# Transposes ahead of two weight chunks in the load queue of a fused LayerNorm + MLP kernel

## Chip, cores, metric

One core of a Trainium2 chip. The metric is the device time of one execution in microseconds (us), median over the runs. The verdicts use runs of the fast state alone. The profile's span is the time from the first to the last instruction; the device time is 1.7 to 2.1 us longer.

## The reference

```python
B, S, D, F = 1, 2048, 1024, 3584          # bf16
def reference(x, w1, b1, w2, b2):
    y = _layernorm(x, axis=-1)
    h = _gelu(jnp.einsum("bsd,df->bsf", y, w1) + b1)
    return jnp.einsum("bsf,fd->bsd", h, w2) + b2
```

## The kernel before

Both matrix products are done as 2x2 block products with seven products instead of eight (Winograd's form), so PE (TensorE) saves an eighth of the work, and DVE (VectorE) pays with sums of blocks of y, w1 and w2. The kernel writes down tasks with dependencies and a due time. A small planner inside it simulates the engines, and so fixes the order of each engine and of the load queue; a packer with a random seed places the buffers.

At the start, y comes into being: 16 tiles of x (128 tokens each) are normalised and transposed. Tiles 0 to 3 are transposed on PE, tiles 4 to 7 by DMA. Until the sums T of y exist, PE can only make products q1 and q2 (which use plain blocks), so it makes them for the first RH = 11 rows of w1, ahead of all else:

```python
RH = 11                    # rows that run ahead of the sums
WAVE_ROWS = 7              # rows in the first wave, token tile by token tile
...
for ch in range((RH + 1) // 2):          # upper half of w1, two rows a chunk, two loads each
    w1_load(0, ch, "A1", (None, W_DUE[ch]) if ch < len(W_DUE) else None)
for i in range(4):
    pr.due = (None, HEAD_LN[i]); norm(i)
... # dummy products keep PE busy
for t in range(4):                       # the first wave: 128-column products
    wave(t, range(0, 3)); ...
    if t < 3: to_yT_pe(0, t + 1, ((7, 0, 8, "ACT", 2),))
    wave(t, range(3, WAVE_ROWS) if t else range(3, 6))
for i in range(4, 8): norm(i)
...
for i in range(4, 8):                    # DMA transposes and the sums T of y
    due(lambda: (to_yT_dma(0, i), tsum(0, i - 4)), HEAD_DUE[0] + HEAD_DUE[1] * (i - 4))()
for r in range(RH):                      # 15 full products: q1 of rows 7-10, q2 of rows 0-10
    if r + 1 >= WAVE_ROWS and r + 1 < RH: p1(r + 1)
    p2(r)
    ...
warm(1, bank=7, full=True)
for ch in range(2):
    if ch == 0: w1_load(0, 0, "A2")      # lower half of w1, first chunk
    w1_sums(0, ch)
# then q6 of row 0, the first product that needs a T and a sum of w1
```

Each `w1_load` is two DMAs of 256 KB. The last product before the sums is q2 of row 10; its weights are the second load of the last upper chunk.

## Time and profile before

| | before |
|---|---|
| device time | 333.53 us median of 3 (333.23 to 334.26) |
| profiled run | 334.5 us, span 332.8 us |
| PE busy | 326.4 us (98%) |
| longest PE wait after the head | 1.42 us, for the sums of y |

The prediction below shows the page's engine row, the chain and PE's timeline. The list of who waited for whom, for PE alone (engine and line, what it waited for: us in total, times, longest), adds that nothing else holds PE after the head:

```profile
PE ps L929 <- DVE mem L758: 1.4, 1, 1.4
PE ps L1301 <- PEq L1596: 0.8, 1, 0.8
PE ps L1346 <- DVE mem L724: 0.5, 1, 0.5
PE ps L1301 <- DVE st_sb L683: 0.4, 1, 0.4
```

L758 is the sums of y, L724 an eviction of tile 0's transpose, L1301 the dummy products.

### The profile page before, as it was taken

How to read it: one execution, taken by the hardware profiler on the slowest of the kernel's cores; microseconds unless marked ns; L12 is line 12 of the kernel's file. 1: busy time of each engine (PE TensorE's matmuls, PEld its weight loads, DVE VectorE, ACT ScalarE, POOL GpSimd, SP SyncE). 2: the span in 40 equal slices, each digit the busy share in tenths (PEclk: the TensorE clock that was granted, in tenths of full speed). 3: DMA queues.
4: the chain of work that ended last, by engine and by line, in shares of the span. 5: the costliest groups of instructions: out<-in, count | busy, mean ns of one | idle time of the engine just before them, and what ended most of it. 6: DMA issues, size and time to landing. Idle time of an engine off the chain costs nothing.

```text
span 332.8 us, 4669 instructions
## 1 busy us (share of the span) xinstructions
PE 326.4 (98%) x1672; PEld 153.9 (46%) x1673; DVE 299.9 (90%) x479; ACT 179.7 (54%) x307; POOL 15.2 (5%) x31
## 2 busy tenths in 40 slices
PE   7998999999999999999999999999999999999996
PEld 4843444444444444444444444444444444444445
DVE  5969999999999986996999997989999999899984
ACT  4795999997577676677675553561211214211411
POOL 2310122111000000000000000000000000000000
PEclk9999999999999999999999999999999999999999
DMA  8998897999998989999967564555689867999768
GB/s 232 323 191 230 246 291 181 301 240 276 306 316 304 318 262 347 315 350 368 320 200 226 152 180 118 161 166 167 175 223 256 228 201 197 279 279 274 186 125 195
DMA packets 121184, 80.73 MB, mean 243 GB/s; under 512 B 35146, under 2 KB 112586, under 8 KB 121162
## 3 DMA queue, kind: packets, MB, share of 16 engines
q1 hardware_dynamic: 118106, 79.32, 84.9%
q10 hardware_dynamic: 3056, 1.11, 1.3%
q8 instruction: 13, 0.21, 0.3%
q14 instruction: 9, 0.07, 0.1%
HBM read 48.70 MB, written 24.38 MB: 220 GB/s over the span
## 4 chain that ended last, share of the span: by engine, by line
PE 90%; SPq 4%; DMA 3%; DVE 1%; issue 0%
PE ps L929 45%; PE ps L1271 44%; SPq L782 3%; DMA mem<-mem 2%; DMA mem<-in_w_dram 1%; DVE mem L758 1%; SPq L653 1%; PE ps L1278 1%; SPq L1319 0%; PE ps L1151 0%; DVE mem L1240 0%; SPq L650 0%; SPq L1320 0%
## 5 line engine op out<-in xcount | busy, mean ns | idle before, releaser
L929 PE MATMUL ps<-mem 128*128 128x512 f16 x756 | 164.1, 379 | 1.4 <-DVE mem L758 1.4
L1271 PE MATMUL ps<-mem 128*128 128x512 f16 x672 | 145.7, 379 | 0.0
L929 PEld LDWEIGHTS ps<-mem 128*128 128x128 f16 (+1 forms) x756 | 73.5, 98 | 91.0 <-DVE mem L758 1.7
L854 ACT COPY mem<-ps 128x512 f32<-128x512 f32 x111 | 64.5, 588 | 75.5 <-PE ps L1271 61.3
L1271 PEld LDWEIGHTS ps<-mem 128*128 128x128 f16 (+1 forms) x672 | 65.7, 98 | 79.3
L838 ACT ACTIVATE mem<-ps,b_sb 128x512 f16<-128x512 f32 x112 | 73.1, 692 | 24.4 <-DVE ps L862 13.8
L862 DVE TENSOR_TENSOR ps<-ps,mem 128x512 f32<-128x512 f32 x84 | 58.0, 693 | 7.4 <-ACT mem L854 4.7
L1086 DVE TENSOR_TENSOR mem<-mem 128x2048 f16<-128x2048 f16 (+1 forms) x56 | 59.3, 1083 | 3.2 <-PE ps L1271 2.4
L794 DVE TENSOR_TENSOR mem<-mem 128x1024 f16<-128x1024 bf16 (+1 forms) x56 | 38.0, 684 | 5.0 <-DMA mem<-in_w_dram 3.6
L995 DVE TENSOR_TENSOR mem<-mem 128x512 f16<-128x512 f16 (+5 forms) x84 | 37.0, 460 | 1.5 <-DMA mem<-in_w_dram 1.1
L1098 DVE TENSOR_TENSOR mem<-mem 128x2048 f16<-128x2048 f16 (+1 forms) x32 | 33.5, 1082 | 1.2 <-PE ps L1271 1.2
L845 ACT COPY ps<-ps 128x512 f32<-128x512 f32 x31 | 17.7, 570 | 24.2 <-DVE mem L1170 15.0
L683 DVE BATCH_NORM_STATS2 st_sb<-mem 128x6 f32<-128x512 bf16 x24 | 15.3, 673 | 3.6 <-DMA mem<-in_x_dram 3.5
L1170 DVE TENSOR_TENSOR mem<-ps,mem 128x512 f32<-128x512 f32 x24 | 16.4, 682 | 1.3 <-PE ps L1271 1.1
L979 DVE TENSOR_TENSOR mem<-mem 128x2048 f16<-128x2048 bf16 (+1 forms) x16 | 17.2, 1077 | 0.1
L1123 DVE TENSOR_TENSOR mem<-ps,mem 128x512 bf16<-128x512 f32 x22 | 14.8, 682 | 0.9 <-PE ps L1271 0.8
L758 DVE TENSOR_TENSOR mem<-mem 128x512 f16<-128x512 f16 x32 | 11.9, 417 | 1.7 <-DMA mem<-mem 1.6
L687 POOL TENSOR_TENSOR rstd_sb<-mv_sb,nhalf 128x1 f32<-128x1 f32 x12 | 8.5, 711 | 45.7 <-DVE mv_sb L685 45.6
L1346 PE MATMUL ps<-mem 128*128 128x128 f16 x112 | 7.3, 219 | 0.6 <-DVE mem L724 0.5
L690 DVE TENSOR_SCALAR mem<-mem,mv_sb,rstd_sb 128x1024 f16<-128x1024 bf16 (+1 forms) x13 | 6.6, 515 | 1.3 <-POOL rstd_sb L687 1.2
L1257 ACT COPY ps<-b_sb 128x512 f32<-128x512 f32 x6 | 3.5, 588 | 7.6 <-DVE mem L1170 7.5
L1346 PEld LDWEIGHTS ps<-mem 128*128 128x128 bf16 x112 | 6.4, 98 | 1.0 <-DVE mem L724 0.7
(45 smaller groups left out, 73.0 us busy)
## 6 DMA issues: line engine op xcount, KB each, us to landing
mem<-in_w_dram SPq DMA_DIRECT2D x80, 256.0 KB, 4.8
mem<-w_scr SPq DMA_DIRECT2D x28, 448.0 KB, 3.8
w_scr<-mem SPq DMA_DIRECT2D x21, 512.0 KB, 5.2
w_raw<-mem SPq DMA_DIRECT2D x12, 512.0 KB, 4.9
mem<-w_raw SPq DMA_DIRECT2D x12, 448.0 KB, 4.4
mem<-in_w_dram SPq DMA_DIRECT2D x9, 448.0 KB, 4.0
mem<-in_x_dram SPq DMA_DIRECT2D x15, 256.0 KB, 4.5
out_dram<-mem SPq DMA_DIRECT2D x12, 256.0 KB, 4.0
```

What stands on the lines that cost most here:

```text
L794: op("DVE", d_tt(n), lambda e: e.tensor_tensor(out=o[0], in0=a[0], in1=bb[0], op=f), r=[a[1], bb[1]], w=[o[1]], name=f"w1S{k}_{ch}")
L838: op("ACT", A_GELU, lambda e: e.activation(out=dst, in_=banks[bank][:, :], func=ACT.Gelu_apprx_tanh, bias=b1_sb[:, f:f + 1], scale=1.0), r ...
L845: op("ACT", A_CP, lambda e: e.copy(out=banks[dst][:, :], in_=banks[src][:, :]), r=[bank_c[src]], w=[bank_c[dst]], name=name, lat=A_LAT)
L854: op("ACT", A_CP, lambda e: e.copy(out=v16(a, 0, 2048, F32), in_=banks[src][:, :]), r=[bank_c[src]], w=[a.c()], name=name, lat=A_LAT)
L862: op("DVE", D_PS, lambda e: e.tensor_tensor(out=banks[dst][:, :], in0=banks[src][:, :], in1=v16(a, 0, 2048, F32), op=ALU.add), r=[bank_c[s ...
L929: i = e.matmul(banks[bank][:, :], lhsT=lv[:, k, :], rhs=rv[:, k, :], start=(fresh and k == 0), stop=(k == KH - 1), skip_group_check=True)
L979: op("DVE", d_tt(2 * self.n), lambda e: e.tensor_tensor(out=vd, in0=va, in1=vb, op=ALU.subtract), r=self.cells(a) + self.cells(bb), w=self ...
L995: tt = lambda o, a, c: (lambda e: e.tensor_tensor(out=o, in0=a, in1=c, op=ALU.subtract))
L1086: op("DVE", d_tt((k1 - k0) * 512), lambda e, a=a, bb=bb, o=o: e.tensor_tensor(out=o, in0=a[0], in1=bb[0], op=f), r=a[1] + bb[1], w=[t.c(z) ...
L1098: op("DVE", d_tt((k1 - k0) * 512), lambda e, va=va, vb=vb, vd=vd: e.tensor_tensor(out=vd, in0=va, in1=vb, op=f), r=h_cells(b, a, s, k0, k1 ...
L1170: op("DVE", D_PS, lambda e: e.tensor_tensor(out=av(dst), in0=banks[bank][:, :], in1=av(src), op=ALU.add), r=[bank_c[bank], src.c()], w=[ds ...
L1271: i = e.matmul(banks[bank][:, :], lhsT=bv[:, k, :], rhs=av3[:, k, :], start=(fresh and k == 0), stop=(k == KQ - 1), skip_group_check=True)
```

## The change

The intent: the transposes of tiles 4 to 7 stood in the queue behind the upper chunks of w1 and the first lower chunk. The last upper chunk and the first lower one now depend on the end of the first wave, so the transposes go first. The head's due times, the planner's price of a transpose, a limit on the planner's queue and the packing seed are tuned with it. The core of the diff (three changes of the same cost factor, to 1.9, are cut to one):

```diff
+BACKLOG = 4.5
...
+                        if e == "SP" and dma_free - now > BACKLOG + 1e-6:
+                            heapq.heappush(events, dma_free - BACKLOG)
+                            break
...
-SEED = 22
+SEED = 18
-HEAD_DUE = (2.0, 1.2)
-HEAD_LN = (4.4, 7.6, 11.1, 12.2)
-TE_DUE = 7.4
-T0_PARTS = ((7, 0, 2, "DVE", 1), (5, 2, 4, "DVE", 1), (6, 4, 8, "ACT", 1))
-W_DUE = (5.5, 9.0)
+HEAD_DUE = (4.0, 2.0)
+HEAD_LN = (3.4, 5.8, 10.2, 14.0)
+TE_DUE = 5.6
+T0_PARTS = ((7, 0, 2, "ACT", 1), (5, 2, 4, "DVE", 1), (6, 4, 8, "ACT", 1))
+W_DUE = (6.2, 7.0)
+W_GATE = (3, 3)
...
-                    ..., P * D * 2 * 1.3, None, f"Td{i}")     # the planner's price of a transpose
+                    ..., P * D * 2 * 1.9, None, f"Td{i}")
...
-            for ch in range((RH + 1) // 2):
+            for ch in range((RH + 1) // 2 - 1):
                 w1_load(0, ch, "A1", ...)
...
                 wave(t, range(3, WAVE_ROWS) if t else range(3, 6))
+                if t == W_GATE[0]:
+                    gate[0] = pr.last_pe
+                    w1_load(0, (RH + 1) // 2 - 1, "A1")
+                    gate[0] = None
+                if t == W_GATE[1]:
+                    gate[0] = pr.last_pe
+                    w1_load(0, 0, "A2")
+                    gate[0] = None
...
-                if ch == 0:
-                    w1_load(0, 0, "A2")
```

More of the change, by code (lines that the diff above doesn't have):

```diff
@@ L740, in to_yT_dma @@
                 dma("SP", lambda e: e.dma_start_transpose(dst, v16(xbuf)),
-                    [xbuf.c(0), xbuf.c(1)], [y[b, c].c((0, t)), y[b, c].c((1, t))], P * D * 2 * 1.3, None, f"Td{i}")
+                    [xbuf.c(0), xbuf.c(1)], [y[b, c].c((0, t)), y[b, c].c((1, t))], P * D * 2 * 1.9, None, f"Td{i}")
                 M.free(xbuf)
@@ L1135, in finish @@
                     dma("SP", lambda e: e.dma_start_transpose(v3(t, 0, t.n, n, BF16), v16(o, 0, o.n, BF16)),
-                        [o.c(0), o.c(1)] if how == "both" else [o.c(dt)], [t.c()], P * o.n * 2.2, None, f"To{i}{k}{u}{v}")
+                        [o.c(0), o.c(1)] if how == "both" else [o.c(dt)], [t.c()], P * o.n * 1.9, None, f"To{i}{k}{u}{v}")
                     M.free(o)
@@ L1222, in part @@
                     pr.due = (pr.last_pe, 8.0)
-                    dma("SP", lambda e: e.dma_start_transpose(v3(tt, 0, 2048, 8), v16(hl)), [hl.c(0), hl.c(1)], [tt.c()], P * 2048 * 2.2,
+                    dma("SP", lambda e: e.dma_start_transpose(v3(tt, 0, 2048, 8), v16(hl)), [hl.c(0), hl.c(1)], [tt.c()], P * 2048 * 1.9,
                         None, f"Td{n}")
```

## The prediction

> **What bounds the kernel now.** I read four views in this order: the busy shares of the page, the chain that ended last, PE's timeline at the head, and the DMA views around the one hole that PE has.
>
> The page's first part says how little there is to win:
>
> ```profile
> PE 326.4 (98%) x1672; PEld 153.9 (46%) x1673; DVE 299.9 (90%) x479; ACT 179.7 (54%) x307; POOL 15.2 (5%) x31
> ```
>
> PE is busy for all but 6.4 us of a 332.8 us span. A busy share can hide slow matmuls, so I check the pace in the chain of waits, asked for its last part and its middle:
>
> ```profile
> 14.77 1.49 SPq L782
> 16.26 0.04 issue
> 16.30 4.64 DMA mem<-in_w_dram
> 20.95 5.37 DMA mem<-mem
> 26.32 0.02 issue
> 26.34 4.19 DVE mem L758 x12
> 30.52 0.05 issue
> 30.57 147.95 PE ps L929 x684
> ...
> 185.65 140.51 PE ps L1271 x651
> ```
>
> 147.95 us / 684 = 216 ns per 128x512 matmul, and 140.51 / 651 = 216 ns too. From 30.57 us on the chain is PE without a hole until the last output tiles at 326; the clock row of the page has nothing but nines. So about 299 us (30.57 to 329.7) cannot shrink by any reordering of loads. Before 30.57 the chain is not PE at all: it runs through the load queue, a w1 load, the transposes of y (mem<-mem), and twelve DVE subtractions. PE's own timeline shows what that costs:
>
> ```profile
> 7.72 0.84 PE L1346 MATMUL ps<-mem 128*128 128x128 f16 x12 [0.51 <-DVE mem L724]
> ...
> 16.04 13.11 PE L929 MATMUL ps<-mem 128*128 128x512 f16 x60
> 30.57 9.67 PE L929 MATMUL ps<-mem 128*128 128x512 f16 x44 [1.42 <-DVE mem L758]
> ```
>
> Three stages: the first wave (128-wide products, 7.72 to 16.04, PE full), 60 full products (16.04 to 29.15, PE full), then 1.42 us of idle until the first product that needs a sum of the transposed tiles 4 to 7. The reachable time is that 1.42 us and what comes before 7.72. This is the whole prize: 1.42 / 333.5 = 0.4%, plus some tenths.
>
> Who holds that hole? The DMA view of 16 to 18 us, of 22 to 24 us and the timeline of the load queue:
>
> ```profile
> DMA packets 1172, 0.58 MB, mean 291 GB/s; under 512 B 36, under 2 KB 1172, under 8 KB 1172
> ```
> ```profile
> 18.04 2.86 SPq L740 DMA_TRANSPOSE mem<-mem  x1
> ...
> mem<-mem SPq DMA_TRANSPOSE x1, 6.8
> ```
> ```profile
> DMA packets 201, 0.05 MB, mean 26 GB/s; under 512 B 201, under 2 KB 201, under 8 KB 201
> ```
>
> The reader is to see that the loads come at 291 GB/s, so a 256 KB load takes 0.9 us; that the first transpose, issued at 18.04, lands 6.8 us later at 24.88 because it stands behind the loads issued before it; and that between 22 and 24 us the DMA engines moved almost nothing (26 GB/s) though transposes were waiting. In the packet records one 16 KB instruction fetch of the other queue ran from 20.64 to 23.16 us (2.52 us; the earlier one, at 14.28, took 1.19), and transpose packets of 18 ns took up to 1.6 us beside it. The landings of the four transposes are 24.88, 26.32, 27.72 and 29.00; when the engines are not held up, one takes about 1.35 us, and alone (issued at 38.62) it lands after 3.3 us.
>
> [...]
>
> **The change part by part.** No arithmetic, no instruction and no byte is removed. It reorders the queue, retunes the priorities of the head and packs the memory anew.
>
> 1. Four loads (the last upper chunk of w1, first needed by product 13 of the 15 before the hole, and the first lower chunk, whose sums feed the product after the hole) no longer stand ahead of the transposes. In front of the first transpose 14 w1 loads become 10: 4 x 0.9 = 3.6 us less queue. The tenth load lands at 18.25 to 19.15 now, so the transposes could move from about 18 us. But they wait for the normalised tiles: DVE's normalisations of tiles 4 to 7 end at 16.0, 17.7, 18.25 and 19.26, with DVE full from 11.5 to 19.3, so they cannot come much earlier. Estimate: landings at 20.5, 21.9, 23.2 and 24.6, which is 4.4 us earlier than now, if the engines are not held up.
> 2. The sums of the tiles (16 x 0.34 us between starts = 5.4 us, of which eight precede the product) then end by about 26.5. That wait is gone: gain up to 1.42.
> 3. The four loads now come after: they are issued from about 20.6, transferred behind the transposes from 24 us, and land at about 25.5, 26.4, 27.3 and 28.2. The upper chunk's product is due at 16.04 + 12 x 0.87 = 26.5: in time with 1 us to spare. The lower chunk needs two sums of 0.69 (1.4 us with their start), so 28.2 becomes 29.6 against 29.15 when PE is free: a hole of 0.4 to 0.5 takes the place of 1.42. Net gain 0.9 to 1.0.
> 4. The head: the first eviction of the first tile's transpose goes from DVE to ACT. Now DVE does both after a 0.68 us statistics instruction, and PE waits 0.51 for the second. In parallel the wave could begin at 7.2 to 7.5. But the next PE transposes wait for the second tile's normalisation, which ends at 8.54 now, and ACT has its own statistics of tile 2 from 6.20 on. I count 0.25 of the possible 0.5. This also lets PE be free 0.25 earlier at the hole, so it counts only if the loads keep up.
> 5. From 30 us on: another queue order and another packing. PE shows no wait at all there now, so nothing can be won, only lost.
>
> Sum of the good case: 333.5 - 0.95 - 0.25 = 332.3. Best case, the hole wholly closed and 0.5 at the head: 333.5 - 1.42 - 0.5 = 331.6.
>
> **The rivals.** First: the wait changes hands. Before the product after the hole the same bytes and the same transposes must have passed, and the queue is full from 2 to 21 us; only the 2.3 us lost at 21.7 to 24 were slack. If the instruction fetch, [...]at about 20.4 us again, meets the transposes again, everything behind it comes 2.3 us later: the last lower load lands at about 29.3 to 30.5, its two sums end at 30.7 to 31.9, and the hole is 1.5 to 2.7, now behind a load; the time is then 333.3 to 334.6. For it: the fetch and the transposes would overlap in time by my own estimate (18 to 24.6). Against it: other transposes are not held up like that, and plain loads at 14.28 lost nothing visible. I give it four in ten, in part or whole.
>
> Second: the loss comes later, because the new order and packing let one of the first products of the next 70 us wait; DVE is busy for 66.4 of 69.4 us from 30.6 to 100, so it has little slack. Such a hole would be some tenths to 2 us: 333 to 335. Against it: PE's list has no wait at all after 32 us, so there is reserve, and the seed of the packing was chosen anew. One in six.
>
> Third: the head does not gain, because ACT's eviction stands behind its 1.1 us statistics, and the wave begins later by up to 0.6; the total stays within 0.3 of now.
>
> **Range and chances.** Weighting: about half for 331.6 to 332.4, four in ten for the hole persisting in part (332.6 to 333.6), the rest above. The middle is 332.4 us. Range 331.3 to 333.9. Faster by over 2% means below 326.9, less than PE's fixed 299 us and the head's 29 with all waits taken out would permit: 1%. Slower by over 2% is above 340.2 and needs 6.7 us of new waits on PE: 2%.
>
> **What would show each step.** Right: the transposes are issued before the last loads, land before 25 us, and PE's wait on the y sums (L758) is gone from the list of its waits; PE's first wave begins before 7.6; the product stage stays at 216 ns. The rival shows as a PE wait of over 1 us ended by the w1 sums (L794) with a DMA of w1 just before, and a stretch at under 50 GB/s near the fetch. The prediction is wrong if PE gains a wait after 32 us, if the first wave gets holes because a w1 chunk comes late, or if the tail after 326 us moves by over 0.3.

What the trace alone shows: 216 ns a matmul in both product stages (that PE can go no faster is not shown); in the first 60 us each transfer of the load queue landed after the one issued before it, so that the first transpose landed at 24.88 us, behind loads at 21.70 and 24.02; 194 GB/s for the transposes (estimate: 256 KB in 1.35 us) against 291 for loads; 418 and 690 ns for DVE's sums of 512 and 1024 columns.

## The result and the profile after

| | before | after |
|---|---|---|
| device time, median of 6 | 333.72 us | 333.91 us |
| range | 333.23 to 334.30 | 332.81 to 334.57 |
| ratio after / before | | 1.0002, 95% interval 0.9981 to 1.0024 |
| span of the profiled run | 332.8 us | 332.8 us |

A ratio is the mean time of one kernel's fast runs over the mean of the other's in the same rounds, so it is not quite the ratio of the medians. The time is unchanged to within noise. The median, 333.91, stands at the very upper end of the predicted range (331.3 to 333.9), and the middle, 332.4, promised 1.1 us that did not come. Where did that microsecond go?

PE's waits in the profile of the changed kernel (line numbers have moved: L934 is the old L929, L763 the old L758, L799 the old L794, L787 the w1 loads, L745 the transposes):

```profile
PE ps L934 <- DMA mem<-in_w_dram: 1.4, 1, 1.4
...
PE ps L1351 <- DMA mem<-in_w_dram: 0.3, 1, 0.3
```

The wait for the sums of y is gone, as intended. A wait of the same length for a load of w1 has taken its place, and a small new one for a w1 load in the first wave. PE's timeline shows where:

```profile
7.61 0.83 PE L1351 MATMUL ps<-mem 128*128 128x128 f16 x12
...
9.57 1.51 PE L1351 MATMUL ps<-mem 128*128 128x128 f16 x24 [0.29 <-DMA mem<-in_w_dram]
...
16.06 12.25 PE L934 MATMUL ps<-mem 128*128 128x512 f16 x56
29.69 148.87 PE L934 MATMUL ps<-mem 128*128 128x512 f16 x688 [1.38 <-DMA mem<-in_w_dram]
```

The first wave began at 7.61 instead of 7.72, lost that again to the load of the third chunk, and was done at 16.06 against 16.04. Then come 56 matmuls, 14 of the 15 products, and the hole of 1.38 us stands before the fifteenth: q2 of row 10. The chain of waits tells why its weights were late (start us, us, what):

```profile
14.62 5.41 DMA mem<-mem
...
23.08 0.70 SPq L745
23.78 0.04 issue
23.82 0.58 SPq L787
...
25.03 4.53 DMA mem<-in_w_dram
29.55 0.14 issue
29.69 1.02 PE ps L934 x4
```

and the load queue in order of time shows what it did:

```profile
14.62 4.31 SPq L745 DMA_TRANSPOSE mem<-mem  x2
18.98 0.58 SPq L787 DMA_DIRECT2D mem<-in_w_dram  x1
19.60 4.18 SPq L745 DMA_TRANSPOSE mem<-mem  x2
23.82 2.82 SPq L787 DMA_DIRECT2D mem<-in_w_dram  x5
```

Two transposes, the first load of the last upper chunk, two transposes, then the rest: the lower chunk (landed 27.19 and 28.01), the load that PE waits for (issued 25.03, landed 29.55), and two of the next lower chunk. The transposes landed at 20.02, 20.97, 24.68 and 25.67, where the kernel before had 24.88, 26.32, 27.72 and 29.00. So they did come 3.0 to 5.4 us earlier. But between the second and the third there is a gap of 3.7 us for one load and one transpose; of the eight transfers before that load and the seven after it, twelve landed 0.7 to 1.0 us after the one before. The DMA view of 22.0 to 23.5 us of the changed kernel:

```profile
DMA packets 191, 0.06 MB, mean 38 GB/s; under 512 B 159, under 2 KB 191, under 8 KB 191
```

and of 17.5 to 19.0 us:

```profile
DMA packets 330, 0.10 MB, mean 66 GB/s; under 512 B 270, under 2 KB 330, under 8 KB 330
```

Two stretches of almost idle DMA, in the packet records about 1.2 us (17.8 to 19.0) and 1.5 us (22.1 to 23.6) long, in a queue whose end PE waits for. This is the first rival of the prediction.

### The profile page after: what moved, and what is told of

Read it like the earlier page. It is cut to its first block, busy times and chain, and to the rows that moved or that the text cites. A ratio compares the mean times of both kernels' runs of the same rounds, so it can differ in the third digit from the quotient of the medians.

```text
span 332.8 us, 4656 instructions
## 1 busy us (share of the span) xinstructions
PE 326.7 (98%) x1672; PEld 154.8 (47%) x1673; DVE 298.9 (90%) x478; ACT 181.0 (54%) x308; POOL 13.7 (4%) x31
## 4 chain that ended last, share of the span: by engine, by line
PE 90%; DMA 5%; DVE 3%; SPq 1%; issue 0%; POOL 0%
PE ps L934 45%; PE ps L1276 44%; DMA mem<-mem 2%; DMA mem<-in_x_dram 2%; DMA mem<-in_w_dram 1%; DVE st_sb L688 1%; PE ps L1283 1%; DVE mem L763 1%; SPq L787 1%; DVE mem L695 0%; SPq L658 0%; POOL rstd_sb L692 0%; SPq L745 0%; DVE mv_sb L690 0%; PE ps L1156 0%
## 5 line engine op out<-in xcount | busy, mean ns | idle before, releaser
L934 PE MATMUL ps<-mem 128*128 128x512 f16 x756 | 164.1, 379 | 1.4 <-DMA mem<-in_w_dram 1.4
L934 PEld LDWEIGHTS ps<-mem 128*128 128x128 f16 (+1 forms) x756 | 73.7, 98 | 90.8 <-ACT mem L843 1.8
L799 DVE TENSOR_TENSOR mem<-mem 128x1024 f16<-128x1024 bf16 (+1 forms) x56 | 37.9, 685 | 1.8 <-DMA mem<-in_w_dram 1.2
L984 DVE TENSOR_TENSOR mem<-mem 128x2048 f16<-128x2048 bf16 (+1 forms) x16 | 17.3, 1082 | 0.0
L763 DVE TENSOR_TENSOR mem<-mem 128x512 f16<-128x512 f16 x32 | 12.1, 419 | 2.5 <-DMA mem<-mem 2.3
L1306 PE MATMUL ps<-const-bfloat16-1.0 128*128 128x128 bf16 (+1 forms) x35 | 6.0, 350 | 1.4 <-PEq L1607 0.8
```

Source lines behind the costliest of these rows:

```text
L799: op("DVE", d_tt(n), lambda e: e.tensor_tensor(out=o[0], in0=a[0], in1=bb[0], op=f), r=[a[1], bb[1]], w=[o[1]], name=f"w1S{k}_{ch}")
L934: i = e.matmul(banks[bank][:, :], lhsT=lv[:, k, :], rhs=rv[:, k, :], start=(fresh and k == 0), stop=(k == KH - 1), skip_group_check=True)
L984: op("DVE", d_tt(2 * self.n), lambda e: e.tensor_tensor(out=vd, in0=va, in1=vb, op=ALU.subtract), r=self.cells(a) + self.cells(bb), w=self ...
```

## Experiments

Two theories of the idle stretches were set against each other. **A:** each turn of the queue from plain loads to transposes costs 1.2 to 2.4 us. **B:** an instruction fetch of 16 KB, which in the records ran at 14.55 (1.19 us long) and at 20.37 (1.79 us), holds up the transposes near it. How it would do so was a guess, not shown. Shown in the packet records of the changed kernel: 18 transpose packets of 256 B, begun from 17.3 to 18.2 us, all ended at 18.99 to 19.03; 17 more, begun from 21.9 to 22.4, all at 23.58 to 23.60. They lasted up to 1.72 us, where the median was 18 ns. Beside them hardly more than one short packet was under way at a time (41 packets with 0.90 us in sum from 18.2 to 18.95). The page lists these fetches as a queue of their own:

```profile
q8 instruction: 13, 0.21, 0.3%
```

Apart from that: how large is the hole in a usual run, and what is it worth?

### No load between the transposes

After planning, the one load between the transposes is moved behind the fourth; nothing else changes.

```diff
+MOVES = (('w100_05', 'Td7'),)
...
             got.schedule(T_PE)
+            sp = got.order["SP"]
+            named = {t.name: t for t in sp}
+            for what, behind in MOVES:
+                named[what].start = named[behind].start + 0.01
```

> The changed kernel, with one load (first half of the last upper chunk) moved behind the fourth transpose in the load queue, so that no load stands between the transposes. Theory A (each turn of the queue from plain loads to transposes costs 1.2 to 2.4 us of near-idle DMA, as at 17.7 to 18.9 and 22.0 to 23.5 us of the changed kernel): the second idle stretch goes, the fourth transpose lands at about 24.0 instead of 25.67, PE's wait for the w1 load falls from 1.38 us to under 0.3, time about 332.6. Theory B (a 16 KB instruction fetch[...]): the idle stretch after the fetch at 20.4 us stays, about 1.5 us long, the fourth transpose lands no earlier than 25.0, PE's wait stays at 1.0 to 1.6, time within 0.3% of before.

Measured: 334.74 us median of 4 against 333.69, ratio 1.0011 (0.9985 to 1.0037): the same. The DMA view from 20.5 to 24.0 us (mean busy share in tenths and GB/s, 40 slices):

```profile
DMA  9999990000001010000039999999999999989973
GB/s 199 184 181 108 53 3 0 0 0 0 0 6 9 6 12 9 9 9 9 12 79 278 293 290 287 264 267 284 260 260 240 231 214 208 190 158 193 234 156 85
```

Four transposes stand in the queue with nothing between them, and still nothing moves from 20.9 to 22.2 us, beside a fetch that ran from 20.18 to 21.51. Theory A's prediction for this stretch fails; B's holds. B was off in the landing (24.50, it said not before 25.0; A said 24.0), and both in the size of PE's wait: 2.1 us, larger, because the first wave ended 0.4 us earlier in this run (15.68) while the load that ends the wait landed no earlier (29.85). It landed no earlier although the fourth transpose was 1.2 us earlier than in the changed kernel: one of the loads after it came 2.21 us after the one before (26.81 to 29.02), with no fetch beside it. What held that one up stays open.

### Instruction fetch earlier

That these fetches are PE's and move with the number of its instructions was assumed for this run and the next, not shown. The times expected are estimates from that: 42 instructions, at two (a weight load and a matmul) in 216 ns, are 4.5 us, and 44 are 4.8.

```diff
             for bank in range(7):
-                warm(1, bank=bank, full=True)
+                warm(4, bank=bank)
```

> The changed kernel with the first seven dummy products cut into four narrow ones each: 42 more PE instructions of the same total time at the start, the same order of every queue; this should bring PE's instruction fetches forward, the one at 20.4 us to about 16. Theory A (turn of the queue): both idle stretches of the DMA stay, near 17.5 and near 22, 1.2 and 1.5 us. Theory B (fetch): the second stretch goes, the first one grows to 2 us or more; the sum, and PE's wait, stay about the same (1.0 to 1.6 us).

Measured: 335.72 against 333.69 us, ratio 1.0052 (1.0032 to 1.0073). The edit did not do what it was made for: only the first fetch moved (to 12.66), the second ran at 20.73 for 0.97 us, and a shorter idle stretch followed, from about 22.5 to 23.3. PE's wait for the load was 0.8 us. Most of what the run lost stands far from the head: in its profile PE waits 1.35 us for DVE at 320.8 us. It fits B's order of size and decides nothing.

### Instruction fetch later

The 28 narrow dummy products become 6 wide ones; the planner is given the old durations, so every queue keeps its order.

```diff
...
-            warm(5)
-            for n, c in ((7, c_st[0][0]), (5, c_mv[0]), (6, c_rstd[0])):
-                warm(n, c)
+            warm(1, full=True, dur=5 * MM128)
+            for n, c, k in ((2, c_st[0][0], 7), (1, c_mv[0], 5), (1, c_rstd[0], 6)):
+                warm(n, c, full=True, dur=k * MM128)
...
-            warm(5, bank=3)
+            warm(1, bank=3, full=True, dur=5 * MM128)
```

> The changed kernel with its 28 narrow dummy products replaced by 6 wide ones: 44 PE instructions fewer, the same order of every queue; the instruction fetch at 20.4 us should move to about 25, after the last transpose. Theory A (turn of the queue): both idle stretches stay, the fourth transpose lands at 25.7. Theory B (fetch): the stretch at 22 to 23.5 goes, the fourth transpose lands at about 24.2; the fetch then sits among plain loads[...], so PE's wait is between 0 and 0.8 us.

Measured: 333.57 against 333.69 us, ratio 0.9993 (0.9975 to 1.0010). The fetch moved further than meant, to 29.99 us. The DMA view of 22.0 to 23.5 us of this run:

```profile
DMA packets 1473, 0.37 MB, mean 248 GB/s; under 512 B 1427, under 2 KB 1473, under 8 KB 1473
```

248 GB/s where the changed kernel had 38, with the same load between the same transposes: the turn from loads to transposes costs nothing here. The fourth transpose landed at 23.93, and PE has no wait between the first wave and 88 us. The time did not fall because PE was slow in the head: the first twelve products took 1.49 us instead of 0.83, and the first wave ended at 16.91 instead of 16.06. The records give a granted clock of 1.00 for that stretch; why the pace was lower is not shown.

### The named move alone

The kernel before, with only the two chunks gated as in the change; seed, head, prices and queue limit stay.

```diff
-            for ch in range((RH + 1) // 2):
+            for ch in range((RH + 1) // 2 - 1):
...
+                if t == 3:
+                    gate[0] = pr.last_pe
+                    w1_load(0, (RH + 1) // 2 - 1, "A1")
+                    w1_load(0, 0, "A2")
+                    gate[0] = None
...
-                if ch == 0:
-                    w1_load(0, 0, "A2")
```

> The kernel before with the named move alone: the last upper chunk and the first lower chunk of w1 are asked for after the first wave; head, seed, cost factors and queue limit as before. If the move alone makes the wait change hands: PE's wait of 1.42 us for the sums of y goes and a wait of 1.0 to 1.8 us for a w1 load or its sums takes its place, time within 0.3% of before. If the new constants are needed for it or hide a gain of it: PE's wait is below 0.8 or above 2.2 us.

Measured: 333.91 against 333.69 us, ratio 1.0003 (0.9988 to 1.0018). The wait changed hands as expected, to a w1 load, but it was only 0.18 us in the profile. Yet the spans of its four runs (331.7 to 332.2) are those of the kernel before on this chip (331.8 to 332.5), because the kernel before has no 1.42 us to give there either. This pointed at the size of the hole, and so to the next two runs. (Its device time is 2.11 us over the span, against 1.74 for the kernel before; why, stays open.)

### Both kernels once more

> The kernel before once more, for a second profile. The profile that the prediction was read from took 334.5 us, 1 us more than the median of its fellows. If the hole in PE is what varies from run to run, a run with a span near 331.9 shows a hole near 0.5 us instead of 1.42, and all else alike to 0.2 us. If the hole is steady, it is 1.3 to 1.5 us again and the difference lies in the head or the tail.

> The changed kernel once more, for a second profile. As above: if the hole varies, it is anywhere from 0 to 1.5 us and the span follows it one for one (331.4 plus the hole); if it is steady, 1.3 to 1.5 us again.

These are single runs, one of each, with a granted clock of 1.00. The kernel before took 333.40 us this time, span 331.7:

```profile
29.62 147.80 PE L929 MATMUL ps<-mem 128*128 128x512 f16 x684 [0.29 <-DVE mem L758]
```

and the changed kernel 333.43, span 331.7:

```profile
28.60 1.02 PE L934 MATMUL ps<-mem 128*128 128x512 f16 x4 [0.54 <-DMA mem<-in_w_dram]
```

The hole is not a property of the kernel, it varies from run to run: 1.42 and 0.29 us before, 1.38 and 0.54 after. The rest is fixed: from the product after the hole to the end it is 302.2 us in one profile of before (332.8 - 30.57) and 302.1 in the other (331.7 - 29.62). The span of a median run of before was 331.9 on the chip of the first experiments, so its hole is about half a microsecond (estimate: 331.9 - 331.7 + 0.29). That was the prize, a third of what the first profile showed.

### Twelve rows ahead instead of eleven

```diff
-RH = 11
+RH = 12
```

> The kernel before, with 12 rows in the group that runs ahead of the sums instead of 11: two more products (1.73 us) that need no load that is not made anyway. If the time that can be had is the hole alone: PE is free only at 30.9 us, after the sums of y are ready at 30.5, so the hole is gone; the median time falls by what the hole is in a median run, about 0.5 us (ratio 0.997 to 0.9995), and the runs lie closer together. If the waits just move on to later products, a hole of over 0.5 us appears elsewhere and the time does not change.

> The changed kernel with 12 rows in the group ahead of the sums: the last products move back by 1.73 us for no further load. If the changed kernel is bound by the w1 loads behind the transposes: PE's wait of 1.38 us for the load goes (that load is wanted at about 28.3 us still, its row's product may be put off), at least to under 0.6, and the time falls by 0.3 to 1.0 us. If not, a wait of over 1 us stays.

Measured: 337.78 us (ratio 1.0121, 1.0100 to 1.0143) on the kernel before and 340.24 (1.0188, 1.0160 to 1.0217) on the changed one, against 333.59. The hole was gone in both: PE has no wait from the first wave to 85 us (before) and to 88 us (after). New ones stand where the old kernels have none; of the kernel before with twelve rows:

```profile
PE ps L929 <- DVE mem L794: 2.7, 2, 2.2
PE ps L1271 <- DVE ps L862: 0.9, 1, 0.9
...
PE ps L929 <- DVE mem L758: 0.6, 1, 0.6
```

and of the changed one with twelve rows:

```profile
247.57 77.16 PE L1276 MATMUL ps<-mem 128*128 128x512 f16 x350 [3.12 <-DMA mem<-w_scr]
```

A row more means other lifetimes, another packing under the same seed, and waits of 0.2 to 3.1 us between 85 and 325 us. In the changed kernel the granted clock also fell to 0.5 for 3.4 us about the end of the long wait (247.1 to 250.5 us; its mean was 0.995 in five of the six runs), which is about 1.7 us of the price (estimate: half of 3.4). My expectation that the gain would simply appear was wrong; its alternative, that the waits move on, came true, at a price of 1.2 to 1.9%.

### One load less before the hole

```diff
                 ch, rr = r // 2, (r % 2) * P
+                if (b, r, q) == (0, 10, 2):
+                    ch = 4
```

The product that waited reads the chunk before its own. The result differs from the reference in principle, though the comparison did not flag it; it is a measurement, not a kernel.

> The changed kernel, wrong on purpose: the last product before the sums reads the weights of the chunk before it, so the load that PE waited for is not needed there, and it goes behind two later loads in the queue. All else is the same. This measures what the whole hole is worth in a median run. If a median run has a hole like that of the first profile (1.4 us): 1.2 to 1.4 us faster than before (ratio about 0.996). If a median run has one like the second profile (0.5 us): 0.3 to 0.6 us faster (ratio 0.998 to 0.999), PE without a wait over 0.3 us from the first wave to the end, span at most 331.4.

Measured: 334.51 against 333.76 us, ratio 1.0023 (1.0006 to 1.0041): not faster, against both expectations. The hole did go: PE's second stage ran from 16.12 without a pause, and the sums' products started at 29.29 instead of 30.77. Then PE waited elsewhere:

```profile
94.82 83.05 PE L936 MATMUL ps<-mem 128*128 128x512 f16 x384 [0.62 <-DVE mem L799]
```

So part of what is won at 29 us is lost again at 95 us, at the sums of w1 on DVE, which in the profile after is busy for 66.2 of the 69.4 us from 30.6 on. This is one profile of one order; the planner had shifted three loads. By the spans (median 332.4 against 332.0) the run lost less than by the device time: 0.3 us of the 0.75 lie outside the span (about 2.1 us against 1.75), as for the named move.

### Fetch late, PE kept busy

The late fetch with two more wide dummies (`warm(2, ...)` first, and two for the second gate); the result is right.

> The run with the late instruction fetch again, with 8 wide dummy products instead of 6[...]; right results. Theory B (fetch): the idle DMA stretch at 22 to 23.5 us is gone again, the fourth transpose lands at 23.5 to 24.3, PE has no hole over 0.3 us before the sums. If the head is then as quick as in the changed kernel (first wave done by 16.1), the span is 331.2 to 331.5 and the time 0.3 to 0.6 us under before (ratio 0.998 to 0.999). If the wide dummies hold PE up, the first wave ends at 16.5 to 17 and the time is that of before.

Measured: 333.01 us, median of 5, against 333.76, ratio 0.9978 (0.9960 to 0.9995). The DMA view of 22.0 to 23.5 us:

```profile
DMA packets 1619, 0.40 MB, mean 270 GB/s; under 512 B 1599, under 2 KB 1619, under 8 KB 1619
```

and PE's timeline:

```profile
16.00 13.11 PE L934 MATMUL ps<-mem 128*128 128x512 f16 x60
29.17 5.34 PE L934 MATMUL ps<-mem 128*128 128x512 f16 x24
34.84 26.07 PE L934 MATMUL ps<-mem 128*128 128x512 f16 x120 [0.33 <-ACT mem L859]
61.46 116.78 PE L934 MATMUL ps<-mem 128*128 128x512 f16 x540 [0.55 <-ACT mem L859]
```

The head is as quick as in the changed kernel, the hole is closed, the fourth transpose landed at 24.04, the fetch ran at 30.15. The spans of the five runs are 331.1, 331.2, 331.3, 331.9 and 332.5; the profile is of the slowest, with two short waits for ACT. Without them it would have been 331.6. This is the only version that measured under the kernel before with an interval clear of 1, by 0.2%. It was not timed beside the changed kernel, which stands at 1.0002 of before.

### The old head in the changed kernel

`HEAD_LN`, `TE_DUE`, `T0_PARTS` and `W_DUE` back to their values of before.

> The changed kernel with the four head constants of the kernel before (norm, eviction and w1 due times, and the first eviction on DVE). If the new head is worth something of its own: the first wave ends 0.1 to 0.3 us later than in the changed kernel (15.8 to 16.1) and the time rises by as much. If the load queue decides, the hole shrinks by what the head loses and the time stays within 0.2 us of the changed kernel, 333.6 to 334.0.

Measured: 334.20 against 333.76 us, ratio 1.0012 (0.9996 to 1.0028). The first wave began at 7.71 and ended at 16.11, in the changed kernel's profiles at 7.61 and 7.59, and 16.06 and 15.82. So the wave ended 0.05 to 0.29 us earlier with the new head, no more than its own two profiles differ (0.24). Whether it reaches the total can't be told: the interval holds 1, and the changed kernel was not in these rounds. The hole here was 0.87 us. The list of waits names ACT, but it was the same load again: it landed at 29.09, and PE began its weights 0.11 us later, as after the load in the changed kernel (0.11 and 0.10).

### The late load first

The load that PE waited for moves ahead of the lower chunk: `MOVES = (('w101_05', 'Td7'),)`.

> The changed kernel with the load that PE waited for moved ahead of the two loads of the lower chunk. If only the order among these three is at fault: no hole, span 331.3 or less. If the queue as a whole is late: the wait changes hands once more, now to the sums of w1 (PE waits for DVE), 0.5 to 2.5 us long, and the span is 331.7 to 333.5.

Measured: 333.56 us, span 331.8, one run, its state unknown. PE's longest wait after the head:

```profile
PE ps L935 <- DVE mem L800: 0.8, 1, 0.8
```

L800 is the sums of w1 here. The wait changed hands once more, to what had been served first, as the second expectation said. In this profile the queue as a whole is late by 0.8 us; its order only picks who tells PE so.

## Why the prediction was right or wrong

**Right: what is fixed.** The product stage stayed at 216 ns (147.79 us for 684 matmuls), and all that moved lay before 31 us. So the class, no change of 2%, was never in doubt.

**Right: the first rival, given four chances in ten.** The wait changed hands with almost its old length, 1.38 for 1.42 us. The fetch met the transposes at 20.37 us, as the rival said ("about 20.4"), and the stretch under 50 GB/s that was to show it is there (38). Size and path were off: it had PE wait 1.5 to 2.7 us for the sums of the lower chunk, and PE waited for the upper chunk's load itself. That the median still falls at the end of the range is owed to the room left for this rival; the middle was missed.

**Wrong: the prize.** "The reachable time is that 1.42 us" took one profile for the kernel. The profiled run was 1 us slower than the median, and the number was in plain sight. The second profile has 0.29, a median run about 0.5. The best case of 331.6 could not have come from there.

**Wrong: step 3, the size of the new hole.** It said 0.4 to 0.5 us for a usual run; 1.38 and 0.54 were measured. The last load that PE needs was to land at 28.2; it landed at 29.55 (28.47 in the second profile). The landing times show which terms were mis-sized in the first profile, against the prediction's 0.9 us a load and 1.3 to 1.4 a transpose:

| landing | predicted us | measured us | late by |
|---|---|---|---|
| second transpose, at | 21.9 | 20.97 | -0.93 |
| the load between the transposes, after it | 0.9 | 2.86 | 1.96 |
| third and fourth transpose | 2.7 | 1.84 | -0.86 |
| first load after them | 0.9 | 1.52 | 0.62 |
| second | 0.9 | 0.82 | -0.08 |
| third, the one PE waits for | 0.9 | 1.54 | 0.64 |
| sum | | | 1.35 |

The largest term is the load beside the second fetch, which was counted at nothing ("if the engines are not held up"). Without a fetch beside it this load took 1.64 and 1.51 us in the two late-fetch runs, so about 1.3 of the 1.96 us are the fetch's (estimate). Against it a transpose was priced too dear: 1.35 us each was the pace of issue in the kernel before (1.32 and 1.34 us for the last two issues); where they stood ready in the queue they landed 0.95 and 0.99 us apart. The first load after transposes lands 1.25 to 1.81 us after the one before it in every profile where no fetch is beside it. It lands 3.3 to 3.7 us after its issue, little more than loads issued to a nearly idle queue (2.6 and 3.2 us), so it seems to be the issue that comes late, behind the issue of the transposes (the last took 1.30 us of the queue, to 23.78, in the first profile). The third load took 0.84 to 2.21 us in the profiles, with no fetch beside it; why stays open. The step also took both loads of the upper chunk to come before the lower chunk, and PE to wait for a sum. The second load came last, so PE waited for a load directly.

**Half right: the head, step 4.** 0.25 us was counted. The wave began 0.11 and 0.19 us earlier (first and second profiles), but its end moved by +0.02 and -0.17, because in the first profile the third chunk's load, with its place in the queue unchanged (landing 9.51 before, 9.53 after), set the pace. That the head's gain "counts only if the loads keep up" was right. This hole of 0.29 us in the first wave is also one of the prediction's own signs of being wrong ("the first wave gets holes because a w1 chunk comes late"). The third rival, a later start of the wave, did not show.

**The second rival** (later waits from another packing) did not show in the changed kernel, whose PE has no wait after 31 us. It is what undid the twelve rows, and part of what undid the shortened queue.

**What is shown and what is not.** Shown: with the fetch moved past 29 us and the queue's order kept, the second idle stretch is gone, twice (248 and 270 GB/s for 38), and a stretch at the fetch stands even where no load is between the transposes. The dummy products were changed with it, so by these runs it is the fetch's time or something else that goes with those dummies; nothing else in the queue differed.

The landing times of the fourteen traces narrow it down. From 9 us to the first fetch, loads in a row land 0.66 to 1.07 us apart. After that fetch one transfer is late in every profile: it lands 1.23 to 2.46 us after the one before it, and 1.1 to 2.0 us after the fetch's end, wherever that lay (at 14.89 us with the fetch at 12.66, 17.58 with 14.55, 18.72 with 15.75). The second fetch does the same in the twelve profiles that have it among these transfers: the next to land comes 2.20 to 3.20 us after the one before, be it a load (2.32 in the first profile of the kernel before) or a transpose (2.38 in the second, with the fetch at 22.47). In the two late-fetch runs the load between the transposes came 1.64 and 1.51 us after the transpose before it; in the seven other profiles with the same order 2.20 to 3.20. So the delay goes with the fetch, and plain loads suffer it too. The prediction's "plain loads at 14.28 lost nothing visible", on which it leaned against its rival, was a misreading: the load at 17.34 came 1.48 us after the one before it, its neighbours 0.9.

Not shown by an experiment: what makes the first stretch, at 17.5 us. It is there in every profile of the changed kernel's order, the late-fetch ones too. In the packet records little but single loads' packets moves then (ten of 512 B in a quarter of a microsecond, 27 to 31 ns each in the first profile), beside the transposes' that stand still. That the fetch at 14 to 15 us had put these loads behind is a guess; no run was without that fetch. Against the first turn from loads to transposes speaks that the first transpose lands 0.82 to 0.88 us after the load before it in all eleven profiles with the transposes ahead: the stretch adds nothing to what the late load before it had lost.

**Figures for the next estimate.** The 16 KB fetches took 0.88 to 2.52 us each in the first profiles of both kernels (13 in each span, one each 24 to 32 us in the product stage). Transposes queued ahead landed 0.79 to 1.09 us apart (256 KB each; a load takes 0.9), in the second profile of the kernel before too (0.86, 0.83, 1.09); where the queue had to issue one after the other, in its first profile, 1.28 to 1.44. The issue of one of 128x1024 took 1.2 to 1.4 us of the queue, up to 3.3 us behind others, against 0.35 to 0.6 for a load on a free queue. Device time less span was 1.74 us for the kernel before and 2.11 us for the named move alone, steady to 0.05 us within each.

## What to carry to other kernels

Before working out what a hole is worth, compare the profiled run's time with the median, and take a second profile: a hole of a microsecond may be one run's luck (1.42 and 0.29 us here). (In four of the experiments, too, the profiled run was the slowest of its kernel.) Reordering a queue that was late as a whole handed the wait to another consumer here (1.42 us for the sums of y, then 1.38 for a load, then 0.8 for the sums of w1); count the work that must have passed before the consumer, and look for stretches where the queue stands still: the one version that measured under the kernel before (0.9978) was one without the second of them. And in a kernel whose order and packing are planned as one, a gain of half a microsecond in one place has to survive the new plan everywhere else.
